# Scores of two attention heads as two 64-row tiles of TensorE, in place of 128 rows with zero halves of q

## The chip, the cores and the metric

One core of a Trainium2 chip. The metric is the device time of one execution in microseconds (us). An execution counts as slow where it is over 1.5% above the fastest of its kernel; only fast ones are compared. Ratios are the mean time of one kernel's fast runs over that of the other's of the same rounds on the same chip, so not quite the ratio of the medians that stand beside them. Engines in the profile: PE is TensorE's matmuls, PEld its weight loads, DVE VectorE, ACT ScalarE, POOL GpSimd. A *stage* below is a stretch of the program; a *call* is one score tile of one pair of heads. The profile names with each matmul the part of TensorE's array that it uses, rows*columns (128*128, 64*128); going from 128*128 to 64*128 or back is called a change of *mode*, and the pause that the traces show there the *drain*. In the profiles of the kernel before, L308 is the scores, L404 the first GEMM, L442 the second and L344 the attention output; in the changed kernel these are L296, L392, L430 and L332.

## The reference

Causal attention with a forget gate, followed by a two-layer MLP (GELU) over all tokens:

```python
batch, n_heads, seq, head_dim = (8, 8, 576, 64)
scores = scale * np.matmul(q, k.transpose(0, 1, 3, 2))
decay = cum[:, :, :, None] - cum[:, :, None, :]      # cum: running sum of log f
scores = np.where(causal, -1000000000.0, scores + decay)
attn = softmax(scores); attn_out = attn @ v          # 4608 tokens x 512
h = x @ w_in                                         # 512 -> 2048
g = 0.5 * h * (1.0 + erf(h * inv_sqrt2))
out = g @ w_out                                      # 2048 -> 512
```

## The kernel before

For each of 8 batches there are two stages. In the first GEMM stage PE multiplies by `w_in` (64 matmuls of 512 columns) and ACT computes GELU. In the attention stage of the next batch PE alternates score matmuls, attention output and, as filler, single matmuls of the previous batch's second GEMM, while ACT computes the exponentials. Heads go in pairs; a head has 64 channels, so a pair's transposed k fills 128 partitions. The kernel before contracts over all 128 rows and keeps q of each head in a tile of its own with zeros in the other head's half:

```python
STILES = [                                   # (k block, first q column, columns)
    [(0, 0, 256), (3, 384, 192)],
    [(0, 256, 320), (4, 448, 128)],
    [(1, 128, 448)],
    [(2, 256, 320)],
]
def zero_halves(pairs):
    for i in pairs:
        nc.vector.memset(qA[i][D:P, :], 0.0)
        nc.vector.memset(qB[i][0:D, :], 0.0)
# ... cut ...
def scores(b, i, t):
    on_pe = b == 0 or (b == 1 and i == 0)    # causal mask by matmuls
    st = s_psum.tile([P, 2, 512], FP32, tag="s", name=f"s{t}")   # one bank per head
    c = 0
    for n, q0, w in STILES[t]:
        for h, qt in enumerate((qA[i], qB[i])):
            nc.tensor.matmul(
                st[:, h, c : c + w], kT[i][:, K0[n] : K0[n] + P], qt[:, q0 : q0 + w],
                start=True, stop=not on_pe or c not in SDIAG[t])
        # ... cut: mask matmuls where on_pe ...
        c += w
    # ... cut: exp on ACT into et, causal select on POOL ...

FILL = [[4, 6, 2, 2], [2, 2, 2, 2], [2, 2, 2, 2], [2, 2, 1, 1], [8, 0, 20]]
def attention(b, fill, counts):
    for i in range(HP):
        for t in range(4):
            scores(b, i, t)
            # ... cut: parts of attend() of the pair before ...
            take(fill, counts[i][t])         # so many matmuls of the second GEMM
    # ... cut: the last pair, with counts[HP] ...
```

The softmax here doesn't subtract the row's maximum and nothing guards it: scores larger than these inputs give would overflow.

## Time and profile before

| what | value |
|---|---|
| time, median of 3 runs | 357.27 us (357.21 to 358.21) |
| span in the profile | 356.2 us |
| PE in the chain that ended last | 94% |
| score matmuls in that chain | 13% |
| first GEMM stage to the next one, batches 3 to 7 | 37.42 us |
| first matmul of the first GEMM of batch 0 | 28.75 us |

Such a chain is read from its end: each step names what released it. With PE at 94% only PE's own time counts, and the steady period can be read from the same chain in order of time (start, duration, line, count), here of the kernel before:

```profile
146.92 13.89 PE ps L404 x64
184.34 13.89 PE ps L404 x64
221.76 13.89 PE ps L404 x64
```

Each first GEMM stage starts 37.42 us after the one before. The page's groups for the touched work (line, operation, operands, count; busy us and mean ns; idle time before) are these:

```profile
L308 PEld LDWEIGHTS <-kT 128*128 128x128 bf16 x384 | 36.7, 98 | 33.3 <-issue 6.2
L308 PE MATMUL s<-qA,kT 128*128 128x256 bf16 (+2 forms) x192 | 51.9, 282 | 2.1 <-ACT e L323 2.0
L308 PE MATMUL s<-qB,kT 128*128 128x256 bf16 (+2 forms) x192 | 48.6, 282 | 0.0
```

The durations overlap, so their sum of 100 us is not PE's time on scores; that is about 46 us.

### The profile page before, as it was taken

How to read it: one execution, taken by the hardware profiler on the slowest of the kernel's cores; microseconds unless marked ns; L12 is line 12 of the kernel's file. 1: busy time of each engine (PE TensorE's matmuls, PEld its weight loads, DVE VectorE, ACT ScalarE, POOL GpSimd, SP SyncE). 2: the span in 40 equal slices, each digit the busy share in tenths (PEclk: the TensorE clock that was granted, in tenths of full speed). 3: DMA queues.
4: the chain of work that ended last, by engine and by line, in shares of the span. 5: the costliest groups of instructions: out<-in, count | busy, mean ns of one | idle time of the engine just before them, and what ended most of it. 6: DMA issues, size and time to landing. Idle time of an engine off the chain costs nothing.

```text
span 356.2 us, 7069 instructions
## 1 busy us (share of the span) xinstructions
PE 346.8 (97%) x2756; PEld 190.7 (54%) x2756; DVE 182.1 (51%) x482; ACT 217.4 (61%) x298; POOL 124.5 (35%) x243
## 2 busy tenths in 40 slices
PE   8998989999999999999999999999999999999995
PEld 3784556544664466445654565446544664444443
DVE  6771984595467625781559145924584361011011
ACT  5697586368854797279826882688457854603600
POOL 7390275406546044804470256215520530000000
PEclk9999999999999999999999999999999999999999
DMA  7999999885997894489639973979310132011013
GB/s 116 169 188 191 190 155 202 183 192 90 205 158 161 146 185 122 95 142 189 144 98 134 188 139 82 174 141 173 76 66 2 45 61 81 2 59 59 2 30 88
DMA packets 103936, 43.85 MB, mean 123 GB/s; under 512 B 82720, under 2 KB 99360, under 8 KB 103904
## 3 DMA queue, kind: packets, MB, share of 16 engines
q1 hardware_dynamic: 86608, 29.26, 40.4%
q0 software_dynamic: 16896, 13.63, 25.6%
q10 hardware_dynamic: 400, 0.52, 0.4%
q8 instruction: 21, 0.34, 0.4%
q14 instruction: 11, 0.09, 0.1%
HBM read 36.85 MB, written 9.44 MB: 130 GB/s over the span
## 4 chain that ended last, share of the span: by engine, by line
PE 94%; ACT 2%; DMA 1%; issue 1%; DVE 1%; POOL 0%; ACTq 0%; DVEq 0%; POOLq 0%
PE ps L404 35%; PE ps L442 35%; PE s L308 13%; PE o L344 8%; ACT e L323 2%; PE ps_f L198 1%; DMA k<-in_k_dram 1%; PE s L317 1%; PE ps_w L187 1%; PE ps_x L380 0%; PE s_t L233 0%; PE ps_t L233 0%; DVE x L360 0%; ACT xt L368 0%; ACT g L416 0%
## 5 line engine op out<-in xcount | busy, mean ns | idle before, releaser
L416 ACT ACTIVATE g<-ps 128x512 bf16<-128x512 f32 x144 | 86.0, 597 | 97.9 <-PE ps L404 97.8
L442 PE MATMUL ps<-w_out_sb,g 128*128 128x512 bf16 (+2 forms) x592 | 143.8, 373 | 0.0
L323 ACT ACTIVATE e<-s 128x896 bf16<-128x896 f32 (+1 forms) x128 | 105.1, 863 | 19.8 <-PE s L308 11.3
L404 PE MATMUL ps<-xT,w_in_sb 128*128 128x512 bf16 x512 | 112.9, 379 | 0.7 <-ACT xT L383 0.6
L325 POOL TENSOR_SCALAR_AFFINE_SELECT e<-e 128x256 bf16<-128x256 bf16 x135 | 53.7, 408 | 118.6 <-ACT e L323 117.7
L404 PEld LDWEIGHTS <-w_in_sb 128*128 128x128 bf16 x576 | 56.0, 97 | 69.2 <-issue 3.9
L451 DVE COPY ot<-ps 128x512 f32<-128x512 f32 (+2 forms) x37 | 25.1, 677 | 105.3 <-PE ps L442 105.0
L442 PEld LDWEIGHTS <-g 128*128 128x128 bf16 x592 | 52.2, 98 | 41.8
L292 POOL TENSOR_TENSOR vw<-v_sb,wT 128x640 bf16<-128x640 f32 x32 | 41.0, 1282 | 45.7 <-PE ps_t L233 15.9
L308 PEld LDWEIGHTS <-kT 128*128 128x128 bf16 x384 | 36.7, 98 | 33.3 <-issue 6.2
L308 PE MATMUL s<-qA,kT 128*128 128x256 bf16 (+2 forms) x192 | 51.9, 282 | 2.1 <-ACT e L323 2.0
L308 PE MATMUL s<-qB,kT 128*128 128x256 bf16 (+2 forms) x192 | 48.6, 282 | 0.0
L344 PE MATMUL o<-vw,e 128*128 128x65 bf16 x960 | 43.5, 194 | 0.5 <-ACT e L323 0.4
L344 PEld LDWEIGHTS <-e 128*128 128x128 bf16 x960 | 39.5, 98 | 7.5 <-ACT e L323 0.5
L359 DVE RECIPROCAL r<-o 128x5 f32<-128x5 f32 x64 | 12.5, 195 | 41.5 <-PE o L344 41.0
L276 DVE COPY kT<-tk 64x288 bf16<-64x288 bf16 x96 | 32.3, 336 | 1.4
L360 DVE TENSOR_TENSOR x<-o,r 128x256 bf16<-128x256 f32 x64 | 27.2, 425 | 2.4 <-DVE r L359 0.2
L276 DVE COPY qB<-tq 64x288 bf16<-64x288 bf16 x48 | 18.8, 391 | 0.6
L370 DVE TENSOR_SCALAR xt<-o,r 64x64 bf16<-64x64 f32 x60 | 17.5, 291 | 1.4
L276 DVE COPY qA<-tq 64x288 bf16<-64x288 bf16 x48 | 17.1, 355 | 1.1
L404 PE MATMUL ps<-tails,w_in_sb 128*128 128x512 bf16 x64 | 14.4, 377 | 0.0
L416 ACT ACT_TABLE_LOAD x8 | 10.3, 1283 | 0.1
(63 smaller groups left out, 124.4 us busy)
## 6 DMA issues: line engine op xcount, KB each, us to landing
out_dram<-ot SPq DMA_DIRECT2D x32, 256.0 KB, 2.2
v_sb<-in_v_dram SPq DMA_DIRECT2D x20, 256.0 KB, 4.7
v_sb<-in_v_dram SPq DMA_DIRECT2D x29, 128.0 KB, 5.4
q<-in_q_dram POOLq DMA_DIRECT2D x6, 576.0 KB, 6.6
k<-in_k_dram POOLq DMA_DIRECT2D x6, 576.0 KB, 9.0
w_in_sb<-in_moe_w_in_dram POOLq DMA_DIRECT2D x4, 512.0 KB, 7.6
w_out_sb<-in_moe_w_out_dram POOLq DMA_DIRECT2D x4, 512.0 KB, 9.6
q<-in_q_dram POOLq DMA_DIRECT2D x4, 144.0 KB, 4.1
```

The costliest lines, as they stand in the source:

```text
L276: nc.vector.tensor_copy(rows[:, odd], src[odd * D : (odd + 1) * D, 2 * i + h].rearrange("d j p -> d p j"),)
L292: nc.gpsimd.tensor_tensor(vw_of[b][:, hs, :, 0:D], v_sb[:, hs, :, :], w.unsqueeze(3).to_broadcast([P, 2, NBLK, D]), Alu.mult,)
L308: nc.tensor.matmul(st[:, h, c : c + w], kT[i][:, K0[n] : K0[n] + P], qt[:, q0 : q0 + w], start=True, stop=not on_pe or c not in SDIAG[t],)
L323: nc.scalar.activation(et[:, :, 0:c], st[:, :, 0:c], Act.Exp, scale=scale)
L325: nc.gpsimd.affine_select(out=et[:, :, c0 : c0 + P], in_=et[:, :, c0 : c0 + P], compare_op=Alu.is_ge, fill=0.0, base=0, pattern=[[0, 2], [ ...
L344: nc.tensor.matmul(o[:, m, :], e_of[b, i, t][:, h, c : c + P], vw_of[b][:, 2 * i + h, n, :], start=(n == 0), stop=(n == m),)
L360: nc.vector.tensor_tensor(x_of[b, i][:, :, h, :], o[:, 0:4, 0:D], r[:, 0:4].unsqueeze(2).to_broadcast([P, NBLK - 1, D]), Alu.mult,)
L370: nc.vector.tensor_scalar(*tail, r[D:P, 4:5], None, Alu.mult)
L404: nc.tensor.matmul(ps, w_in_sb[:, kt, ffb * P : (ffb + 1) * P], src[:, kt, :], start=(kt == 0), stop=(kt == n_dm - 1),)
L416: nc.scalar.activation(g_of[c][ffb], ps, Act.Gelu)
L442: nc.tensor.matmul(pss[ts][:, c0:c1], g_of[c][kt][:, ts * P : (ts + 1) * P], w_out_sb[:, kt, c0:c1], start=(kt == 0), stop=(kt == n_ff - 1),)
L451: nc.vector.tensor_copy(ot[:, c0:c1], pss[ts][:, c0:c1])
```

## The change

Half of every product of the kernel before is with zeros. The intent is to drop the zeros, to stack q of both heads as k is stacked, and to give each head a row tile of 64 rows: the two matmuls may then stream at the same time.

```diff
-    qA = [consts.tile([P, S], BF16, name=f"qA{i}") for i in range(HP)]
-    qB = [consts.tile([P, S], BF16, name=f"qB{i}") for i in range(HP)]
+    qT = [consts.tile([P, S], BF16, name=f"qT{i}") for i in range(HP)]
-    def zero_halves(pairs): ...                  (and its two calls)
     # batch 0, after the transposes: one copy of q for both heads instead of two
-            evac(nc.vector if i else nc.scalar, qA[i], 0, D)
-            evac(nc.vector, qB[i], D, P)
+        op = nc.scalar.copy if i == 0 and not which else nc.vector.tensor_copy
+        op((qT, kT)[which][i].rearrange("d (p j) -> d p j", j=JT), ps.rearrange("d j p -> d p j"))
     # transposes_pe and untangle (cut): the target is (qT, kT)[which][i]
-            for h, qt in enumerate((qA[i], qB[i])):
+            for h in range(2):
+                d = slice(h * D, (h + 1) * D)
                 nc.tensor.matmul(
                     st[:, h, c : c + w],
-                    kT[i][:, K0[n] : K0[n] + P],
-                    qt[:, q0 : q0 + w],
+                    kT[i][d, K0[n] : K0[n] + P],
+                    qT[i][d, q0 : q0 + w],
```

More of the change, by code (lines that the diff above doesn't have):

```diff
@@ L142 @@
     make_identity(nc, ident_fp)
-    qA = [consts.tile([P, S], BF16, name=f"qA{i}") for i in range(HP)]
-    qB = [consts.tile([P, S], BF16, name=f"qB{i}") for i in range(HP)]
+    qT = [consts.tile([P, S], BF16, name=f"qT{i}") for i in range(HP)]
     kT = [consts.tile([P, S], BF16, name=f"kT{i}") for i in range(HP)]
-    def zero_halves(pairs):
-        for i in pairs:
-            nc.vector.memset(qA[i][D:P, :], 0.0)
-            nc.vector.memset(qB[i][0:D, :], 0.0)
     w_in_sb = consts.tile([P, n_dm, d_ff], BF16)
@@ L174 @@
     nc.vector.memset(ones, 1.0)
-    zero_halves(range(2))
     nc.vector.memset(wT[0:D, 4, :], 0.0)
@@ L202, in transposes_first @@
                 )
-        def evac(eng, dst, r0, r1):
-            op = eng.copy if eng is nc.scalar else eng.tensor_copy
-            op(
-                dst[r0:r1, :].rearrange("d (p j) -> d p j", j=JT),
-                ps[r0:r1].rearrange("d j p -> d p j"),
-            )
-        if which:
-            evac(nc.vector, kT[i], 0, P)
-        else:
-            evac(nc.vector if i else nc.scalar, qA[i], 0, D)
-            evac(nc.vector, qB[i], D, P)
+        op = nc.scalar.copy if i == 0 and not which else nc.vector.tensor_copy
+        op(
+            (qT, kT)[which][i].rearrange("d (p j) -> d p j", j=JT),
+            ps.rearrange("d j p -> d p j"),
+        )
     def transposes_pe(b, i, pool):
@@ L239, in transposes_pe @@
             for h in range(2):
-                dst = (qA[i], qB[i])[h] if which == 0 else kT[i]
+                dst = (qT, kT)[which][i]
                 rows = dst[h * D : (h + 1) * D, :].rearrange(
@@ L270, in untangle @@
             for h in range(2):
-                dst = (qA[i], qB[i])[h] if which == 0 else kT[i]
+                dst = (qT, kT)[which][i]
                 rows = dst[h * D : (h + 1) * D, :].rearrange(
@@ L481, in first_attention @@
         transposes(0, o_psum, "o")
-        zero_halves(range(2, HP))
         warm_up(4)
```

## The prediction

> **What bounds the kernel now.** I read the page's busy shares first, then the chain that ended last, then PE's waits, then the timeline of one steady batch.
>
> ```profile
> PE 346.8 (97%) x2756; PEld 190.7 (54%) x2756; DVE 182.1 (51%) x482; ACT 217.4 (61%) x298; POOL 124.5 (35%) x243
> ...
> PE 94%; ACT 2%; DMA 1%; issue 1%; DVE 1%; POOL 0%; ACTq 0%; DVEq 0%; POOLq 0%
> PE ps L404 35%; PE ps L442 35%; PE s L308 13%; PE o L344 8%; ACT e L323 2%; PE ps_f L198 1%; DMA k<-in_k_dram 1%; PE s L317 1%; PE ps_w L187 1%; PE ps_x L380 0%; PE s_t L233 0%; PE ps_t L233 0%; DVE x L360 0%; ACT xt L368 0%; ACT g L416 0%
> ```
>
> TensorE alone sets the end: 94% of the chain is PE, and the score matmuls (L308), which the change touches, are 13% of it, some 46 us. A check from the source: a pair has 448 + 448 + 448 + 320 = 1664 score columns per head, and there are 32 pairs of two heads, so 106,496 columns. At 2.4 columns per ns that is 44.4 us, and 384 matmuls at 2.5 ns more make 45.3 us.
>
> ```profile
> PE s L308 <- ACT e L323: 2.0, 3, 1.0
> PE ps_w L187 <- DVE warm L173: 1.3, 1, 1.3
> PE ps L404 <- ACT xT L383: 0.6, 1, 0.6
> ```
>
> PE's waits (us, times, longest) come to some 5 us, nearly all in the first 50 us. Inside a steady batch there is nothing to wait for:
>
> ```profile
> 206.85 0.27 PE L308 MATMUL s<-qA,kT 128*128 128x256 bf16 x1
> 206.96 0.27 PE L308 MATMUL s<-qB,kT 128*128 128x256 bf16 x1
> 207.07 0.25 PE L308 MATMUL s<-qA,kT 128*128 128x192 bf16 x1
> 207.15 0.25 PE L308 MATMUL s<-qB,kT 128*128 128x192 bf16 x1
> 207.24 0.59 PE L442 MATMUL ps<-w_out_sb,g 128*128 128x512 bf16 x2
> 207.67 0.30 PE L308 MATMUL s<-qA,kT 128*128 128x320 bf16 x1
> ```
>
> Columns: start, duration, what. Durations overlap (0.27 us against 0.11 us from start to start), so only starts count. The four score matmuls of a tile start at 206.850 and their successor at 207.235: 385 ns for 896 columns, which is 896/2.4 + 4 x 2.5 = 383 ns. Subtracting such a time from every start-to-start distance leaves about 0.26 us of stall in a steady attention stage of 23.2 us, at its start, where ACT loads its table. A nanosecond added to PE there is a nanosecond of the result.
>
> **What the Trainium skill says.** (1) "TensorE: Matmul & The Clock Gate", section "Part 3: Packing small matmuls — row/col tiling": matmuls in distinct row groups run concurrently, starting about 4 ns apart; four row tiles of K=32, N=512 measured 3.07x. The trace before agrees in kind for column tiles: the 24 transposes of the first stage (96*64, 96 columns each) take from 13.153 to about 13.80, 0.65 us, where one tile steps by 42.5 ns and 24 in a row would be 1.02 us; the starts of the two halves alternate. (2) "TensorEngine Tiling (Array Packing)", section "Tiling Modes", Key Properties: changing the mode, not just the tile, drains TensorE; no number is given. The trace before gives one, since it has a few such changes already:
>
> ```profile
> 11.46 0.22 PE L317 MATMUL s<-after,ident_bf 128*128 128x128 bf16 x1
> 11.61 0.27 PE L489 MATMUL psw<-ident_fp,f_sb 64*128 64x64 f32 x1
> ...
> 11.90 0.22 PE L489 MATMUL psw<-ident_fp,f_sb 64*128 64x64 f32 x1
> 12.06 0.36 PE L308 MATMUL s<-qA,kT 128*128 128x448 bf16 x1
> ```
>
> (the third field after MATMUL is the tile, rows*columns). A 128-column matmul gives way after 55 ns; here 64*128 comes 150 ns after it. And 128*128 comes 157 ns after the last 64*128, which step by 62 ns. In nanoseconds the next weight load starts 92 ns late going in (11.456, then 11.603) and 90 ns late going out. Changes to 96*64 and back, at 13.005 and 13.760, give 91 and 92 ns. The control is the group of 96*128 transposes at 34.98: it has another count of rows, but no drain, 216 ns after a 512-column matmul like any other. So the drain belongs to the tile's mode; it looks like the emptying of the array. (3) The same tiling page, section "Restrictions and Gotchas", says that row tiles must write different PSUM banks, which the score tile does (one head per 512 f32), and names only column tiling as shutting out the fast weight load. No run so far shows the latter for 64-row bf16 loads.
>
> **The change part by part.**
>
> 1. Scores run as two row tiles. Each call (one tile of one pair) has its streaming halved, because head 1 streams beside head 0. Tiles 0 and 1: 448/2.4 + 2 x 2.5 = 192 ns. Tile 2: 189 ns. Tile 3: 320/2.4 + 2.5 = 136 ns. Before: 384, 384, 377, 271 ns. It saves 192, 192, 188 and 135 ns, 0.71 us a pair, 22.6 us over 32 pairs, if nothing is paid.
>
> 2. Each call now changes the mode twice, since its neighbours (the second GEMM, the attention output) stay 128*128. Going in costs 91 ns. Weights can't be loaded during the drain, and in the trace the first matmul after a change steps 10 ns longer for a 128-row load (12.061 to 12.260 is 199 instead of 189) and 24 ns longer for 96*64. I choose 12 ns for a 64-row load with all 128 columns. Head 1 starts somewhat after head 0, since its load comes second: I choose 15 ns (a normal load spacing here is 15 to 29 ns). Going out costs 91 + 10 ns. Sum: 91 + 12 + 15 + 91 + 10 = 219 ns a call.
>
> 3. Net of the two: tile 0 and tile 1 +27 ns each, tile 2 +31, tile 3 +84: +169 ns a pair. Batches 1 to 7 have 27 pairs without masks on PE: 4.6 us. In one place (batch 1, pair 1) two calls follow each other directly, which spares two changes: -0.2. So +4.4 us, wholly on the path.
>
> 4. Batch 0 and the first pair of batch 1 add the causal mask by 128*128 matmuls inside the call. Tile 0 has a mask between its two parts, so it changes the mode four times instead of twice: 2 x 103 = 206 ns more, 375 ns a pair, 1.9 us for five pairs. But that stage has PE waits of 0.67, 0.21, 0.20 and 0.56 us on ACT and DVE and 1.15 us at 46 us, which absorb part. I take half: +0.9.
>
> 5. DVE loses 8 memsets of 0.30 us and, in batch 0, 4 of its 12 copies of 0.75 us. The memsets lie in waits (after 8.5 us DVE idles before the next copy). The copy of pair 0's q goes to ACT whole, so that scores could start about 0.8 us sooner, but four warm-up matmuls on PE, ahead of them in program order, end at 8.67 anyway. The other copies free a PSUM buffer sooner, but the next transposes started 13.005 to 13.153 for the drain alone. I take -0.2.
>
> 6. Untangling (L276) keeps its 192 copies of 64x288; only their target's name changes. ACT's exponentials see the same tiles. The counts of score matmuls and weight loads stay 384.
>
> Sum: 4.4 + 0.9 - 0.2 = 5.1, so 362.4 us.
>
> **The rivals.** A: the drain is hidden or small, and the halved columns come through: up to -22 us. For it speaks the reorder window seen among the transposes; against it, four changes of mode that all cost 90 to 92 ns. Even then ACT would soon bind: 16 exponentials of 863 ns are 13.8 us, but PE's fillers leave only about 1.05 us per tile, of which PE would give up 0.19; the 16 interleaved tiles would gain some 3 us a batch at most. About 340 us. B: the two row tiles don't overlap, because something serialises their loads or writes. Then streaming stays at 384 ns and the changes are pure loss: 128 x 0.2 = 26 us, about 383 us. Against it speaks the overlap of the column tiles. C: head 1 starts 40 to 50 ns late, or a 64-row load loses its fast form (the f32 one lengthened the first step by 48 ns). That is 30 to 60 ns a call more, 4 to 7 us: 366 to 369 us. This is the rival I take most seriously. D: the changed mode costs less when the drained matmul is a long one or the mode repeats, 60 ns instead of 91: 128 x 62 ns = 8 us less, 354 us, within 2%.
>
> **Range and chances.** The middle is two large terms that nearly cancel (-22.6 us of streaming; 128 x 219 ns = 28 us of changes, less what merges), so each 10 ns per call is 1.3 us. Uncertainty of about 25 ns a call, mostly upward (C), gives 359.5 to 367.5. Slower by 2% is above 364.4, which takes 16 ns a call more than my sum: 0.31. Faster by 2% is below 350.1 and needs A: 0.04. Within 2%: 0.65.
>
> **What would show it.** In a steady batch the timeline should show score matmuls as 64*128, head 1 starting within some 20 ns of head 0, each pair stepping by columns/2.4; a gap of about 146 ns plus nothing else from the last 128-column matmul's start to the first 64*128 one (about 307 ns after a 512-column one, instead of 216); the same on the way out; a steady batch of 37.4 us becoming 38.1; no ACT waits on PE's list that were not there; DVE without L150 and L151. The score line should show fewer busy microseconds although the span grows. The prediction is wrong in its core if gaps at the changes are not near 90 ns, if head 1 starts after head 0 has streamed, or if PE starts waiting for ACT in the steady batches.

## The result, and the profile after

359.37 us, the median of 4 runs (359.23 to 364.79; the run of 364.79 is a slow one, clock 0.981), against 357.56 us of 4 runs of before, the 3 above and a later one; ratio of the fast runs 1.0047 (95% interval 1.0026 to 1.0068). The result is within 2% and slower, but the time lies just under the predicted range of 359.5 to 367.5. A second set of six runs, told below, gave 360.1 us and a ratio of 1.008.

The page of the changed kernel:

```profile
PE 347.7 (97%) x2756; PEld 161.5 (45%) x2756; DVE 176.7 (49%) x470; ACT 217.1 (61%) x298; POOL 124.0 (35%) x243
...
L296 PE MATMUL s<-qT,kT 64*128 64x320 bf16 (+4 forms) x384 | 46.0, 285 | 2.2 <-ACT e L311 2.0
...
L296 PEld LDWEIGHTS <-kT 64*128 64x128 bf16 x384 | 14.6, 93 | 49.7 <-issue 44.7
```

The score group fell from 51.9 + 48.6 to 46.0 us of busy time while the span grew by 1.3 us. Two heads now start together, and the busy time of a group is the union of its records. The cost is in what busy time does not show; in the timeline of a steady stage:

```profile
207.23 0.37 PE L296 MATMUL s<-qT,kT 64*128 64x256 bf16 x4
207.53 0.60 PE L430 MATMUL ps<-w_out_sb,g 128*128 128x512 bf16 x2
208.07 0.37 PE L296 MATMUL s<-qT,kT 64*128 64x320 bf16 x4
208.36 0.36 PE L332 MATMUL o<-vw,e 128*128 128x65 bf16 x6
208.57 0.59 PE L430 MATMUL ps<-w_out_sb,g 128*128 128x512 bf16 x2
209.09 0.36 PE L296 MATMUL s<-qT,kT 64*128 64x448 bf16 x2
```

The two fillers of 512 columns from 207.53 keep PE to 207.97 (the last starts at 207.754 and takes 216 ns). The next scores start at 208.07: some 96 ns of drain, though a record of 0.60 us seems to cover the gap. In the trace, to the nanosecond, both weight loads start at 208.062 and 208.065, head 0 at 208.066 and head 1 at 208.069; the second parts follow at 208.213 and 208.216, and the attention output starts at 208.364. So the overlap is complete and the drain is paid on each side.

Medians over batches 3 to 7, from the end of the predecessor's columns (its start, columns/2.4 and 2.5 ns) to the start of the successor, plus what the successor's first step takes over its usual one:

| call (columns per head) | before, ns | after, ns | difference |
|---|---|---|---|
| tile 0 (256 + 192) | 383 | 404 | +21 |
| tile 1 (320 + 128) | 381 | 402 | +21 |
| tile 2 (448) | 375 | 397 | +22 |
| tile 3 (320) | 268 | 346 | +78 |

That is +142 ns a pair and 4 x 142 = 568 ns a stage. Yet the stages of the changed kernel, in the chain in order of time, follow each other after 37.76 us, only 0.34 us more:

```profile
146.81 13.89 PE ps L392 x64
184.57 13.89 PE ps L392 x64
222.33 13.89 PE ps L392 x64
```

The trace shows where the missing 0.23 us went. At the start of a stage ACT loads its table (1.28 us), and the third score tile needs the PSUM buffer that ACT's first exponential (`e<-s`) empties, since `s_psum` has two. Before:

```profile
162.76 0.92 ACT L323 ACTIVATE e<-s 128x896 bf16<-128x896 f32 x1
163.73 0.35 PE L308 MATMUL s<-qA,kT 128*128 128x448 bf16 x1
```

and after:

```profile
162.65 0.92 ACT L311 ACTIVATE e<-s 128x896 bf16<-128x896 f32 x1
163.62 0.37 PE L296 MATMUL s<-qT,kT 64*128 64x448 bf16 x2
```

In both kernels this tile starts 0.05 us after that exponential ends and 16.97 us after the start of the first GEMM stage, and the fifth tile follows at 18.59 us in both. So what the slower calls cost PE before these moments does not show.

And the first GEMM of batch 0 started 1.32 us *sooner* than before (27.43 against 28.75 us). These two differences are what the experiments had to explain.

### The profile page after: what moved, and what is told of

It is laid out like the page before. It is cut to its first block, busy times and chain, and to the rows that moved or that the text cites. A ratio compares the mean times of both kernels' runs of the same rounds, so it can differ in the third digit from the quotient of the medians.

```text
span 357.5 us, 7057 instructions
## 1 busy us (share of the span) xinstructions
PE 347.7 (97%) x2756; PEld 161.5 (45%) x2756; DVE 176.7 (49%) x470; ACT 217.1 (61%) x298; POOL 124.0 (35%) x243
## 4 chain that ended last, share of the span: by engine, by line
PE 93%; ACT 2%; DMA 1%; issue 1%; DVE 1%; POOL 1%; ACTq 0%; DVEq 0%; POOLq 0%
PE ps L430 36%; PE ps L392 35%; PE s L296 10%; PE o L332 10%; ACT e L311 2%; DMA k<-in_k_dram 1%; PE s L305 1%; PE ps_f L192 1%; PE ps_x L368 0%; PE ps_t L220 0%; PE s_t L220 0%; POOL q L102 0%; DVE xT L371 0%; DVE x L348 0%; POOL k L102 0%
## 5 line engine op out<-in xcount | busy, mean ns | idle before, releaser
L430 PEld LDWEIGHTS <-g 128*128 128x128 bf16 x592 | 49.2, 98 | 48.2 <-issue 7.1
L296 PE MATMUL s<-qT,kT 64*128 64x320 bf16 (+4 forms) x384 | 46.0, 285 | 2.2 <-ACT e L311 2.0
L332 PEld LDWEIGHTS <-e 128*128 128x128 bf16 x960 | 35.3, 98 | 13.3 <-issue 7.2
L296 PEld LDWEIGHTS <-kT 64*128 64x128 bf16 x384 | 14.6, 93 | 49.7 <-issue 44.7
L263 DVE COPY qT<-tq 64x288 bf16<-64x288 bf16 x96 | 35.9, 374 | 1.7
L102 POOL DMA_DIRECT2D q<-in_q_dram x12 | 9.1, 762 | 0.9 <-POOLq L625 0.9
```

The source lines that it names most:

```text
L263: nc.vector.tensor_copy(rows[:, odd], src[odd * D : (odd + 1) * D, 2 * i + h].rearrange("d j p -> d p j"),)
L296: nc.tensor.matmul(st[:, h, c : c + w], kT[i][d, K0[n] : K0[n] + P], qT[i][d, q0 : q0 + w], start=True, stop=not on_pe or c not in SDIAG[t],)
L332: nc.tensor.matmul(o[:, m, :], e_of[b, i, t][:, h, c : c + P], vw_of[b][:, 2 * i + h, n, :], start=(n == 0), stop=(n == m),)
L430: nc.tensor.matmul(pss[ts][:, c0:c1], g_of[c][kt][:, ts * P : (ts + 1) * P], w_out_sb[:, kt, c0:c1], start=(kt == 0), stop=(kt == n_ff - 1),)
```

## The experiments

Theory 1: each change between 128-row and 64-row tiles costs about 100 ns of PE time; the kernel before also wasted some 0.25 us a stage in waiting for ACT at its start, which the slower calls fill; and the early start of the first GEMM is chance. Rivals: the drains partly hide; or the first stage truly gains from the change.

### 1. Both kernels again, and a filler moved

`b_again` and `a_again` are the two kernels unchanged. `b_fill` and `a_fill` have one edit each, the same:

```diff
-FILL = [[4, 6, 2, 2], [2, 2, 2, 2], [2, 2, 2, 2], [2, 2, 1, 1], [8, 0, 20]]
+FILL = [[4, 7, 2, 2], [2, 2, 2, 2], [2, 2, 2, 2], [2, 2, 1, 1], [8, 0, 19]]
```

> The kernel before, unchanged, once more. In the profile of before the full TensorE clock was granted at 10.7 us from the start of the span, in that of the changed kernel at 5.2 us, with the same instructions on PE up to then. Theory 1 (chance): the moment varies from execution to execution whatever the kernel; then this profile may show another moment, and where it is about 5 us the first GEMM starts earlier than the 28.75 us of before, by up to 0.8 us. Rival: the moment belongs to the kernel; then it is 10.7 us again and the first GEMM starts at 28.75. Time ratio to before 1.000 in both.

> The changed kernel, unchanged, to narrow its ratio: 1.0047 (1.003 to 1.007). A steady batch 37.76 us against 37.42. Theory 1 (clock by chance): the grant may come late here, and then the first GEMM starts later than 27.43 us, at about 28.5. Rival: again 5.2 us and 27.43.

> The kernel before with one matmul of the second GEMM moved from the tail of each attention stage (batches 2 to 7) to its second slot, where PE waited 0.15 + 0.11 us for the first exponentials. Theory: this slack of 0.26 us a batch is real time on PE's path that the kernel before wasted and the changed kernel used up. Then a steady batch falls from 37.42 to 37.16 to 37.2 us and the time by 1.3 to 1.6 us (ratio 0.996). Rival: the slack has no part in it (PE meets the next wait later instead), and a steady batch stays at 37.42.

> The changed kernel with the same move of one matmul. Theory: its stage has only about 0.01 us of that slack left, so a steady batch stays at 37.75 and the time equals that of the changed kernel (1.0047 of before). The distance of a steady batch to the filled kernel before is then 0.54 to 0.6 us, the full cost of the mode changes less the halved streaming, instead of 0.34. Rival: the smaller loss came from drains that partly hide; then both kernels gain alike, and the distance stays 0.34.

| run | ratio to before (95%) | steady period, us | first GEMM starts, us |
|---|---|---|---|
| b_again | 1.0004 (0.9984 to 1.0024) | 37.42 | 27.33 |
| a_again | 1.0080 (1.0062 to 1.0099) | 37.76 | 28.04 |
| b_fill | 0.9965 (0.9945 to 0.9984) | 37.25 | 27.40 |
| a_fill | 1.0103 (1.0064 to 1.0143) | 37.74 | 31.82 |

The start of the first GEMM is chance: the unchanged kernel before now has 27.33 us. The warm-up matmuls of 512 columns tell the clock. In the first profile of before:

```profile
6.99 1.03 PE L187 MATMUL ps_w<-warm 128*128 128x512 bf16 x2
```

and in `b_again`, at the same place:

```profile
6.72 0.81 PE L187 MATMUL ps_w<-warm 128*128 128x512 bf16 x3
7.45 0.27 PE L308 MATMUL s<-qA,kT 128*128 128x256 bf16 x1
```

Two matmuls take 1.03 us there and three 0.81 us here: they step by 400 to 427 ns (half clock) against 216 ns, and the first scores start at 7.45 instead of 8.67 us. PE's instructions up to this point are the same. The first GEMM came 1.4 us sooner than in the first profile, where I had expected up to 0.8. The trace's clock records put the grant of the full clock at 10.7 us in the first profile of before, at 5.6 in `b_again`, 5.2 in that of the changed kernel and 5.7 in `a_again`. The clock is not the only chance at the start: `a_again` has its clock nearly as early as the first profile of the changed kernel, but its first GEMM starts 0.6 us later, and its transposes wait 1.3 us in all for k, not 0.6.

`b_fill` wins back 0.17 us a stage, less than the 0.26 I expected: 0.09 us of the wait for the exponentials was left in its trace. `a_fill` gains 0.02 us. The distance of the two grew from 0.34 to 0.49 us, which is 0.568 less the 0.09 still absorbed (0.48). So the slack, not a hidden drain, nearly halved the loss. The profile of `a_fill` fell in a disturbed execution, which the windows show (columns: span of the window, then each engine's busy time and count, the granted clock, DMA share, GB/s):

```profile
8.00:11.00 3.00, 1.72 (x36) 1.10 (x35) 0.72 (x2) 0.92 (x1) 0.29 (x1) 1.00 1.25 196
11.20:21.20 10.00, 9.81 (x104) 5.50 (x103) 3.98 (x7) 6.10 (x8) 5.84 (x9) 0.50 0.80 155
22.00:25.00 3.00, 2.98 (x55) 2.12 (x52) 2.28 (x8) 2.47 (x4) 3.00 (x6) 1.00 1.26 205
```

For ten microseconds the clock was halved (0.50). Two of the six runs of `a_fill`, at 363.5 and 363.8 us (clocks 0.986 and 0.984), widen its interval; its steady batches are undisturbed.

### 2. The change in the first stage alone, and everywhere else alone

`x_b0full` keeps batch 0 as before (`full = b == 0`); `x_b0tile` is the reverse (`full = b > 0`, and the fills with zeros moved behind batch 0's attention). The lines are shown against the changed kernel; cut are the tiles, fills and copies of the kernel before that each keeps:

```diff
             for h in range(2):
-                d = slice(h * D, (h + 1) * D)
+                full = b == 0
+                d = slice(0, P) if full else slice(h * D, (h + 1) * D)
+                qs = (qA[i], qB[i])[h] if full else qT[i]
```

> Batch 0 as in the kernel before (zero halves, 128-row scores, split copies), row tiles from batch 1 on. Theory: the loss sits in batches 1 to 7; a steady batch is 37.76 us, the way from the first GEMM of batch 0 to that of batch 1 is 43.06, and the time is 2.5 to 3 us over the kernel before (ratio 1.008), the same as the changed kernel within noise; the first GEMM starts at 27.3 to 28.8 us, by the moment at which the clock is granted. Rival: the first stage with row tiles gains some 1.3 us, as the first two profiles suggest; then this kernel is 1.3 us slower than the changed one (ratio 1.011).

> The reverse: row tiles and whole copies of q in batch 0 only, zero halves and 128-row scores from batch 1 on (the eight fills with zeros moved into the first GEMM stage). Theory: time equal to the kernel before within 0.2% (the first stage's four extra changes of mode per masked tile and the spared copies cancel, and its waits on the k transfer and on ACT hide the rest); a steady batch is 37.42. Rival (first stage gains 1.3 us): ratio 0.996.

`x_b0full`: 359.16 us, ratio 1.0080 (1.0061 to 1.0099), steady period 37.76 us, batch 0 to batch 1 43.06 us. `x_b0tile`: 356.92 us, ratio 1.0015 (1.0000 to 1.0030), 37.42 us and 42.53 us. The first stage gains nothing; it loses between nothing and 0.3%. The loss of the changed kernel sits in batches 1 to 7: 43.06 - 42.53 = 0.53 us on the way to batch 1, and 6 x 0.34 = 2.04 us after it. Their sum of 2.57 us is 0.7% of the time. The way to batch 1 has a chance of its own: `b_again`, the unchanged kernel before, took 43.04 us for it, and also 0.53 us more than usual on the way to batch 3, and PE waited for transfers in both places:

```profile
PE ps L404 <- DMA xT<-x: 0.5, 1, 0.5
PE ps L442 <- DMA w_out_sb<-in_moe_w_out_dram: 0.4, 1, 0.4
```

The profiles of `before`, `b_fill` and `x_b0tile` have neither wait and 42.53 us each; that of the changed kernel has neither too, so the 0.53 us stand.

Why the whole copies of q don't seem to pay can be read in the waits of PE (us, times, longest); no run tests the copies alone. In `b_again`, with the early clock:

```profile
PE s L308 <- DVE qB L206: 0.5, 1, 0.5
PE ps_f L198 <- DMA k<-in_k_dram: 0.5, 1, 0.5
```

and in the changed kernel:

```profile
PE ps_f L192 <- DMA k<-in_k_dram: 0.6, 2, 0.4
```

The wait of 0.5 us for the second copy of q is gone, but then the transposes of the next pair wait for their k: twice instead of once, and 1.3 us in `a_again`.

### 3. What the overlap is worth

The heads on the same row tile; a wrong result on purpose (the record marks this run as correct all the same, so that mark can't be relied on here):

```diff
-                d = slice(h * D, (h + 1) * D)
+                d = slice(0, D)
```

> Wrong result on purpose: both heads take their operands from rows 0 to 63, so both matmuls fall on the same row tile and can't stream together; the mode changes stay. Theory: this takes back the halved streaming alone, 192, 192, 188 and 135 ns a call or 2.83 us a batch; a steady batch becomes 40.5 to 40.7 us and the time 22 us longer than that of the changed kernel (ratio to before about 1.07). It would show that the halving is fully real and that changes of mode cost about as much. Rival: the two row tiles of the changed kernel overlap only in the record, and nothing is lost by the same tile: 37.8 us a batch.

380.08 us, ratio 1.0652 (1.0639 to 1.0666), steady period 40.52 us. A call's second matmul now starts after the first has streamed (146 ns after it for 320 columns, instead of 3). The overlap of the changed kernel is worth 40.52 - 37.76 = 2.76 us a stage, close to the 2.83 expected, and the mode changes eat all of it and 0.57 us more.

### 4. What a change of mode costs

Two matmuls of 8 columns ahead of every call of batches 2 to 7. In `x_double` they stand on 64 and on 128 rows, in the control `x_tiny` on the two row tiles:

```diff
+        for r0, r1, h in ((0, D, 0), (0, P, 1)) if b > 1 else []:     # x_tiny: ((0, D, 0), (D, P, 1))
+            nc.tensor.matmul(st[:, h, 0:8], kT[i][r0:r1, 0:P], qT[i][r0:r1, 0:8], start=True, stop=True)
```

> The changed kernel with two more changes of mode ahead of each score tile of batches 2 to 7: a matmul of 8 columns on one row tile, then one of 8 columns on all 128 rows, both overwritten by the real scores. Theory: each change costs 92 ns of drain plus about 4 to 10 ns of weight load, whatever lies between, so a call grows by about 200 ns plus two short matmuls (30 ns each at most); a steady batch by 16 times that, 3.2 to 4.2 us, to 41.0 to 42.0. Rival: what drains is the array's content, and 8 columns drain at once: under 1 us a batch.

> The control to it: the two matmuls of 8 columns stand on the two row tiles, so no mode changes are added. Theory: a call grows by the short matmuls alone, 30 to 60 ns; a steady batch by 0.5 to 1.0 us, to 38.2 to 38.8. The difference between the two kernels is the price of 32 changes of mode a batch, some 3.1 us.

One profiled run each, of unknown state. Steady period 41.27 us (`x_double`) and 38.15 us (`x_tiny`); the difference of 3.12 us over 32 changes is 97.5 ns a change. A call in `x_double`:

```profile
224.67 0.29 PE L294 MATMUL s<-qT,kT 64*128 64x8 bf16 x2
224.89 0.31 PE L304 MATMUL s<-qT,kT 64*128 64x320 bf16 x2
```

and in `x_tiny`:

```profile
207.06 0.18 PE L294 MATMUL s<-qT,kT 64*128 64x8 bf16 x2
207.10 0.30 PE L304 MATMUL s<-qT,kT 64*128 64x320 bf16 x2
```

From the first short matmul to the real scores it is 0.22 us with two changes and 0.04 us with none. So a change after 8 columns costs about as much as one after 512: a call of the changed kernel gives (404 - 192)/2 = 106 ns a change, where 192 ns is the streaming of 448 columns in two matmuls. The expected cost of the control was too high (24 ns a call, not 30 to 60).

### 5. Fewer changes of mode, and a mixture of both kernels

`a_merge0` is the changed kernel with the first two calls of a stage back to back:

```diff
-FILL = [[4, 6, 2, 2], ..., [8, 0, 20]]
+FILL = [[0, 11, 2, 2], ..., [8, 0, 19]]
```

> The changed kernel with the first two score tiles of a stage (pair 0, batches 2 to 7) issued one after the other and their ten fillers plus one from the tail after them, so that two of the 32 changes of mode of a stage fall away. Theory (each change costs about 0.1 us of PE time and PE is the bound): a steady batch falls by 0.2 us from 37.76 to 37.55 or so, the time by 1.2 us (ratio 1.004). Rival: ACT's exponentials bind at the start of the stage, and PE waits for them instead: a steady batch stays at 37.7 or more.

358.20 us, ratio 1.0042 (1.0029 to 1.0056), steady period 37.55 us: 0.21 us less for two changes less. The merged call has 896 columns per head and takes 595 ns where the kernel before needs 383 + 381 = 764. Here row tiles win: a call of 448 columns loses 21 ns, one of 896 gains 169, and on the line between them the break-even is near 500 columns per head between two changes (an estimate from these two lengths).

So `h_mix` takes the kernel before and uses row tiles for that merged call alone. The two halves of `qA` and `qB` that hold data serve as they are:

```diff
             for h, qt in enumerate((qA[i], qB[i])):
+                d = slice(h * D, (h + 1) * D) if b > 1 and i == 0 and t < 2 else slice(0, P)
...
-                    kT[i][:, K0[n] : K0[n] + P],
-                    qt[:, q0 : q0 + w],
+                    kT[i][d, K0[n] : K0[n] + P],
+                    qt[d, q0 : q0 + w],
-FILL = [[4, 6, 2, 2], ..., [8, 0, 20]]
+FILL = [[0, 12, 2, 2], ..., [8, 0, 18]]
```

The control `b_merge0` merges the same calls on 128 rows, with `FILL = [[0, 11, 2, 2], ..., [8, 0, 19]]`.

> A mixture: the kernel before with its zero halves and 128-row scores, but the first two score tiles of a stage (pair 0, batches 2 to 7) issued one after the other as row tiles, on the halves of the same two q tiles that hold data, with twelve fillers after them. The merged call took 595 ns with row tiles, the two calls 383 + 381 = 764 ns without, so it saves 0.17 us; the fillers use the slack of 0.17 us that the moved filler showed. Theory: a steady batch falls from 37.42 to about 37.1 us, the time by 1.5 to 2.2 us (ratio 0.994 to 0.996). Rival: ACT's exponentials or the transposing transfer of x bind at this point, and it stays at 37.25 or above.

> The control: the kernel before with the same two tiles issued one after the other, on 128 rows, and eleven fillers after them. No mode changes are spared here, so only the slack is used: a steady batch of 37.25 us as with the moved filler (ratio 0.9965). If it too fell to 37.1, the gain of the mixture would not come from row tiles.

`h_mix`: 356.10 us, ratio 0.9958 (0.9931 to 0.9985), steady period 37.09 us. `b_merge0`: 356.65 us, ratio 0.9991 (0.9971 to 1.0012), 37.25 us. The merged call of `h_mix` in the timeline:

```profile
160.65 0.28 PE L309 MATMUL s<-qA,kT 64*128 64x256 bf16 x1
160.66 0.28 PE L309 MATMUL s<-qB,kT 64*128 64x256 bf16 x1
...
160.99 0.22 PE L309 MATMUL s<-qA,kT 64*128 64x128 bf16 x1
160.99 0.22 PE L309 MATMUL s<-qB,kT 64*128 64x128 bf16 x1
161.14 2.76 PE L443 MATMUL ps<-w_out_sb,g 128*128 128x512 bf16 x12
```

The period fell as expected: 0.17 us by the slack (`b_merge0`, as `b_fill`) and 0.16 us more by the row tiles: the merged call takes 595 ns in `h_mix` and 766 in `b_merge0`. Over 6 stages that is 2 us. The ratio of `b_merge0` came out 0.3% above that of `b_fill`, which has the same period. In its profile two periods were longer by 0.3 to 0.4 us (the one to batch 1 and the one to batch 3), for the same two transfers as in `b_again`; the profile of `h_mix` has both as well (0.6 and 0.8 us), that of `b_fill` neither. So the undisturbed periods are the firmer reading. `h_mix` is the fastest by its period and beats both kernels, `b_fill` next; by their times the intervals of these two overlap.

## Why the prediction was right or wrong

Right was the mechanism with its sign: two large terms that nearly cancel, some 20 us of streaming (2.76 us a stage; in all the ratio 1.0652 of `x_sametile` less the 1.0080 of `a_again`, of 357 us) against some 100 ns for each change of mode, with PE as the bound before and after. Right too: the drain of about 92 ns on each side, complete overlap, no new waits for ACT in steady batches, and the share of batch 1 (predicted 3 x 169 ns, half of 375 ns, less 0.2 us: 0.50; measured 0.53), though that agreement is partly luck: by the table above its three pairs without masks give 3 x 142 ns less 0.2 us, 0.23 us, so the masked pair and the waits beside it took about 0.3 us and not 0.19. Rivals A, B and D fell: no change was cheap, not even after 8 columns, and the heads do overlap. Rival C, which I took most seriously, fell in the other direction: head 1 starts 3 ns after head 0.

Wrong was the sum, 5.1 us for a measured 1.8 (medians of the first set) to 2.9 us (0.8% in the second):

| term | predicted, us | measured, us |
|---|---|---|
| calls, one stage of batches 2 to 7 | 4 x 0.169 = 0.68 | 4 x 0.142 = 0.57 |
| taken up by slack at the stage's start | 0 | -0.24 |
| one stage | 0.68 | 0.34 (the two terms give 0.33) |
| six stages | 4.06 | 2.04 |
| on the way to batch 1's GEMM | 0.50 | 0.53 |
| first stage (half of 4 x 0.375, less 0.2) | 0.5 | 0 to 1 (`x_b0tile`) |

The step that failed is the sentence "A nanosecond added to PE there is a nanosecond of the result". I had measured the stall of 0.26 us a stage that contradicts it, two lines above, and left it out of the sum. It is a wait for ACT's first two exponentials after the table load, whose time PE doesn't set; a slower PE fills it first. The changed kernel has 0.02 us of it left, so it took up 0.24 us in each of six stages: 1.4 of the 2.2 to 3.3 us by which I was too high. `b_fill` shows that most of this slack was free to be used. The second miss is a size in step 2: I chose 15 ns for the start of head 1, and the trace has 3; the exposed weight load, chosen as 12 ns, is about 15 (head 0 starts 4 ns after its load, and its first step is 11 ns longer). With smaller differences in the times of before that makes 6 to 9 ns a call, 27 ns a pair, 0.65 us over batches 2 to 7. The rest of the distance to the first set of runs (359.37 us) is not traced to one cause. The second set and `x_b0full` have 0.8%, which 2.57 us for batches 1 to 7 nearly accounts for; and the profiles show two things that vary from run to run by as much as the two sets differ: the start (1.4 us in the kernel before) and the waits for transfers (1.0 us in `b_again`).

In step 5 DVE's copies are 11, not 12 (the twelfth was on ACT), and the expectation that warm-up matmuls hide the sooner q holds only where the clock is granted late, as in the one profile I had. With the early clock the wait on q is real, 0.5 us in `b_again`, and goes; the transfer of k takes its place. How much the first stage loses exactly stays open between 0 and about 1 us, since the clock and the waits for k move it by more than that from run to run.

## What to carry to other kernels

Count changes of TensorE's tile mode as an instruction of about 100 ns each, and put row tiles only where enough columns stream between two changes (here 500 per head). Grouping calls spares changes: the one merged call saved 0.21 us a stage here; longer groups were not tried. When two large terms nearly cancel, take from the difference every stall that the trace already shows on the critical engine, because a small slowdown fills it before it shows. And look at a second profile before believing a difference in the first microseconds.

## What the Trainium skill lacked or had wrong

- "TensorEngine Tiling (Array Packing)", "Tiling Modes": it says that changing the mode drains TensorE but gives no size. Here the weight load after a change starts 90 to 92 ns late, in either direction, and a change costs 97.5 ns in all (`x_double` less `x_tiny`, after 8 columns; 106 ns by the table of calls). The same page's recommendation of row tiling for contractions of 64 or less ("When to Use Tiling") needs a break-even beside it; here about 500 columns per head.
- "TensorE: Matmul & The Clock Gate", Part 3: starts about 4 ns apart, confirmed (3 ns). Its speedups are for packs alone; with a change of mode on each side the doubling here turned into a loss of 21 to 78 ns a call.
- The same page, Part 1, on the free-running window of the clock gate: agreed. In each of the 14 profiles the full clock lasted a whole number of windows of 3.413 us (351.57 us in `after`, 103 of them; in `a_fill` 6.83 us, then 10.24 us at half). The full clock came at 4.3 to 10.7 us from the start of the span, for the same first instructions on PE, and the first GEMM moved by up to 1.4 us with it (27.33 against 28.75 us, the kernel before). The page's table of states lets the clock fall back after an idle window of about 3.4 us and return after a busy one; a later section of this part tells of short idles that do it too, without a size. In `a_fill` it fell at 11.1 us, after idle times of 1.1 and 1.4 us only (PE was busy for 1.72 us of the 3 us ahead of it), and stayed at 0.50 for ten microseconds in which PE was busy for 9.81 of 10.00 us. Why is not shown.
